# Fused attention and two dense stages: the loads of token units 2 and 3 moved behind those of units 0 and 1, into the space of the second activation tile

## The chip, the cores and the metric

The kernel runs on one core of a Trainium2 chip. The metric is the device time of one execution, in microseconds (us); less is better. Engines are named as in the profile: PE (TensorE, with PEld for its weight loads), DVE (VectorE), ACT (ScalarE), POOL (GpSimd), SP (the engine that issues all loads here), and a trailing q for an engine's sequencer (SPq).

## The reference

Inputs are r, k, v, w of 4 batches x 8 heads x 768 tokens x 48, a vector u of 8 x 48, and five weight arrays. First a recurrence over the tokens of a batch row, per head:

```python
for t in range(S):
    cur = np.einsum('bhd,bhe->bhde', u[None] * kt, vt)
    y[:, :, t] = np.einsum('bhd,bhde->bhe', rt, state + cur)
    state = wt[:, :, :, None] * state + np.einsum('bhd,bhe->bhde', kt, vt)
```

Its output, 3072 tokens x 384, goes through two dense stages:

```python
h = x @ w_in;  x = (h - np.tanh(h)) @ w_out                      # 384 -> 2048 -> 384
h = x @ w_in2; solu = h * softmax(h)                             # 384 -> 1024
out = (layernorm(solu) * g_ln) @ w_out2                          # 1024 -> 384
```

## The kernel before, in words

**Units, blocks, slices.** The recurrence is done in NU = 24 units of 128 tokens. UB = 4 units make a block of 512 tokens, the width of a matmul of the first dense stage; there are NB = 6 blocks. The first dense stage's weights are cut into NM = 16 slices.

**A unit.** `att_load` (L187) has SP load w, r, k into a tile `rkw` (L194, three loads) and v into one of four tiles `vt` (L195). There are two `rkw` tiles, so unit u + 2 is loaded once unit u has been read. `att_pre` has ACT look whether all w are in the range for which the method is safe (`check_w`, L234, two operations that use the tile `inv` as scratch), POOL multiply r, k and u (L243, L244, also in `inv`), and DVE sum (L245). `att_0` transposes w and r on PE (L260), runs four scans on DVE (L274), a logarithm and an exponential on ACT (L277, L278) and a product on DVE (L279). `att_1` has POOL multiply into `inv` (L286), PE transpose k, DVE do L287 and L288. `att_2` is a matmul (L301), a masked copy on DVE (L303, two) and a transpose (L307, copied by ACT, L308). `att_3` is a matmul (L317, L318) and the update of the running state on DVE: L327 adds the matmul's result in PSUM to the old state, L328 multiplies that by a factor, both of its inputs in SBUF. `att_4` is the output matmul (L340, L343).

**The hand-over to the dense stage.** The output of a unit goes into the block's activation tile `xs` as a high and a low part. Three quarters are written there by ACT (L345) and DVE (L347). The last quarter goes to a small tile `x3` (ACT L346, DVE L348) and from there by six SP copies (L351) to other partitions of `xs`. There is one `x3`, so the next unit's L346 waits until the six copies have landed. There are two `xs` tiles; the second is first used by unit 4.

**Weights.** `conv_a` takes a slice: SP loads a raw pair of w_in and w_out, stored as 64-bit numbers (`load_pair`: L361, L362 twice each, L366) into one of two raw buffers; ACT checks it (L121); DVE turns it into 32-bit numbers (L129, L130, L131, twice each); ACT and POOL split that into high and low parts `wa` (L134, L135).

**The dense stage.** `part1` of a block and a slice is nine matmuls `hp` (L381), then ACT L386, DVE L387 (`y`), ACT L390, DVE L392 (`y`), ACT L393, ACT or POOL a cast and POOL the low part of `g` (L398). `part2` is nine matmuls `x2p` (L405). Two PSUM banks hold `hp`.

**What sets the order.** All work is written in one program order, from which a scheduler makes each engine's queue. Until the first block is complete the order comes from a list `first` of (time, function, unit), sorted by time: stage k of unit u stands at k + 2.1 u, the loads of units 2 and on at their own times, and `conv_a` of slices 0 and 1 (`early` = 2) at 0 and 2. After that a loop over s does one `part1`, at most one stage of a unit from 4 on, one `part2` and one `conv_a` (slice s + 2) per step.

## Time and profile before

| | |
|---|---|
| three runs | 786.26, 782.85, 785.9 us (median 785.9) |
| the profiled execution | 782.14 us, of which the span is 780.3 |
| mean granted TensorE clock | 0.985 |
| PE busy | 731.3 us, 94% of the span |
| DVE, ACT, POOL busy | 582.5 (75%), 495.0 (63%), 419.7 us (54%) |
| moved by DMA | 113.12 MB, mean 145 GB/s |

The span goes from the first to the last instruction that the profile shows; the execution's own time is 1.8 us longer. A PE that is busy in nearly all of a stretch is what limits that stretch, so what matters is where PE is not busy. The 40 slices of the page are 19.5 us each; PE's digits are 3, 6, 7, 7 and 9 in the first five, and 9 in nearly all others.

### The profile page before, as it was taken

Reading aid. Unit: us, or ns where it says so; the run is one execution under the profiler, and the core shown is the slowest. Engines: PE = TensorE matmul, PEld = TensorE weight load, DVE = VectorE, ACT = ScalarE, POOL = GpSimd, SP = SyncE. Lnnn points to the kernel's source line nnn. Section 1 sums busy time; section 2 is a strip of 40 time slices with the busy share of each in tenths; the row PEclk is TensorE's granted clock in tenths of the full one; section 3 lists DMA queues with packets and bytes.
Section 4 is the critical chain, followed back from the end, with each engine's and each line's share of the span. In section 5 each row is a group of like instructions: output and inputs, shape, how many; then the busy total and the mean of one; then the engine's idle time right before and its main releaser. Section 6 shows DMA issues by size and latency. Waiting matters only on the chain. (4 is left out here: it accounts for less than half of the span.)

```text
span 780.3 us, 13211 instructions
## 1 busy us (share of the span) xinstructions
PE 731.3 (94%) x4338; PEld 605.5 (78%) x4338; DVE 582.5 (75%) x1023; ACT 495.0 (63%) x944; POOL 419.7 (54%) x389
## 2 busy tenths in 40 slices
PE   3677989899999999999999999999999999999996
PEld 2565767678887888887887887887778999998986
DVE  4688989776776677766676765468569899999992
ACT  3434777487776777686777765697745554554552
POOL 3444657466565656646555655367425444545440
PEclk9978999999999999999999999999999999999999
DMA  9964674778587568657665630043035555645531
GB/s 164 184 101 116 132 179 122 169 176 206 127 182 184 137 152 184 172 145 205 158 158 162 178 88 25 25 143 121 5 130 184 178 172 168 195 161 171 184 108 46
DMA packets 178158, 113.12 MB, mean 145 GB/s; under 512 B 95520, under 2 KB 166816, under 8 KB 178080
## 3 DMA queue, kind: packets, MB, share of 16 engines
q1 hardware_dynamic: 178080, 112.19, 55.5%
q8 instruction: 36, 0.59, 0.3%
q14 instruction: 42, 0.34, 0.1%
HBM read 88.81 MB, written 20.97 MB: 141 GB/s over the span
## 5 line engine op out<-in xcount | busy, mean ns | idle before, releaser
L405 PE MATMUL x2p<-g,wa 128*128 128x512 f32 x864 | 223.9, 398 | 4.0 <-ACT g L395 2.8
L381 PE MATMUL hp<-xs,wa 128*128 128x512 f32 x864 | 216.9, 395 | 5.5 <-DVE y L392 5.0
L381 PEld LDWEIGHTS hp<-xs,wa 128*128 128x128 f32 x864 | 162.5, 190 | 43.1 <-POOL wa L135 7.0
L405 PEld LDWEIGHTS x2p<-g,wa 128*128 128x128 f32 x864 | 158.1, 188 | 42.6 <-issue 4.2
L398 POOL TENSOR_TENSOR g<-y,g 128x512 fp32r<-128x512 f32 x96 | 128.6, 1340 | 42.7 <-ACT g L395 33.3
L387 DVE TENSOR_TENSOR y<-hp,t 128x512 f32<-128x512 f32 x96 | 65.9, 687 | 81.3 <-ACT t L386 65.5
L393 ACT ACTIVATE q<-t,cst 128x512 f32<-128x512 f32 x96 | 69.4, 723 | 65.6 <-DVE y L392 65.1
L462 PE MATMUL h<-wb,x2s 128*128 128x512 f32 x432 | 103.8, 392 | 3.0 <-POOL x2s L451 1.4
L544 PE MATMUL o<-wb,ts 128*128 128x384 f32 x576 | 105.1, 336 | 1.0 <-POOL ts L523 1.0
L544 PEld LDWEIGHTS o<-wb,ts 128*128 128x128 f32 x576 | 100.8, 188 | 3.0 <-POOL ts L523 1.3
L462 PEld LDWEIGHTS h<-wb,x2s 128*128 128x128 f32 x432 | 80.6, 188 | 20.0 <-POOL x2s L451 1.9
L397 POOL TENSOR_SCALAR g<-y 128x512 fp32r<-128x512 f32 x64 | 40.3, 630 | 91.9 <-DVE y L392 65.4
L386 ACT ACTIVATE t<-hp 128x512 f32<-128x512 f32 x96 | 56.5, 589 | 26.1 <-PE hp L381 25.4
L523 POOL TENSOR_TENSOR ts<-tw,ts 128x512 fp32r<-128x512 f32 x44 | 57.9, 1339 | 7.5 <-ACT ts L522 7.4
L392 DVE SCALAR_TENSOR_TENSOR y<-q,y 128x512 f32<-128x512 f32 x64 | 49.9, 780 | 4.4 <-ACT q L390 1.2
L451 POOL TENSOR_TENSOR x2s<-x2s 128x384 fp32r<-128x384 f32 x24 | 24.9, 1040 | 49.9 <-ACT x2s L450 49.9
L495 ACT ACTIVATE e<-so 128x1024 f32<-128x1024 f32 x24 | 25.5, 1060 | 37.2 <-DVE so L494 37.2
L390 ACT ACTIVATE q<-t,cst 128x512 f32<-128x512 f32 x64 | 46.2, 722 | 1.2
L519 DVE STREAM_TRANSPOSE tw<-sw 128x1024 f32<-128x1024 f32 x22 | 45.0, 2046 | 2.6 <-DMA sw<-dso 2.4
L286 POOL TENSOR_TENSOR inv<-inc,kh 112x512 f32<-112x512 f32 x24 | 29.7, 1236 | 32.0 <-ACT kh L278 25.9
L135 POOL TENSOR_TENSOR wa<-cv_x,wa 128x768 fp32r<-128x768 f32 x16 | 29.4, 1839 | 29.7 <-ACT wa L134 29.7
L301 PEld LDWEIGHTS qk<-rh,kh 48*128 48x128 f32 x384 | 28.0, 200 | 18.8 <-issue 12.3
(134 smaller groups left out, 1208.1 us busy)
## 6 DMA issues: line engine op xcount, KB each, us to landing
raw<-in_moe_w_out_dram SPq DMA_DIRECT2D x48, 384.0 KB, 4.4
dso<-so SPq DMA_DIRECT2D x22, 512.0 KB, 3.0
sw<-dso SPq DMA_DIRECT2D x88, 128.0 KB, 3.0
raw<-in_moe_w_in_dram SPq DMA_DIRECT2D x64, 144.0 KB, 3.6
rkw<-in_r_dram SPq DMA_DIRECT2D x64, 96.0 KB, 2.7
rkw<-in_k_dram SPq DMA_DIRECT2D x64, 96.0 KB, 2.5
rkw<-in_w_dram SPq DMA_DIRECT2D x64, 96.0 KB, 3.3
raw<-in_moe_w_in_dram SPq DMA_DIRECT2D x16, 384.0 KB, 3.6
```

The costliest lines, as they stand in the source:

```text
L381: self.mm(hp, self.wa[:, a, m, j * 128:(j + 1) * 128], xs[:, b, j], start=n == 0, stop=n == len(seq) - 1)
L386: nc.scalar.activation(t, hp, AF.Square)
L387: v.tensor_tensor(y, hp, t, ALU.mult)
L390: nc.scalar.activation(p, t, AF.Square, bias=self.c_fsb, scale=F_S)
L392: self.last_dve = v.scalar_tensor_tensor(y, p, F_E, y, ALU.add, ALU.mult)
L393: self.last_act = nc.scalar.activation(q, t, AF.Relu, bias=self.c_t2, accum_out=self.flags[:, col:col + 1])
L398: g.tensor_tensor(gs[:, 1], y, gs[:, 0], ALU.subtract)
L405: self.mm(self.x2p[d], self.wa[:, a, m, sl], gs[:, b], start=m == 0 and n == 0, stop=m == NM - 1 and n == 2)
L462: self.mm(p[:, f], xs[:, a, j], w, start=q == 0, stop=q == 8)
L519: self.turned = nc.vector.transpose(x.rearrange("p k (t b) -> p b k t", b=4), sw)
L523: nc.gpsimd.tensor_tensor(ts[:, 1, k], x[:, k], ts[:, 0, k], ALU.subtract)
L544: self.mm(p, ts[:, a, k], self.wb[:, b, k, DM:], start=q == 0, stop=q == 3 * NM2 - 1)
```

## The change

Units 0 to 3 get an `rkw` tile each: two more are made in the space in which the second `xs` tile is made later, at unit 4's `att_4` (the tag `xs1`). The loads of units 2 and 3 stand right behind those of units 0 and 1, and the raw pairs of slices 0 and 1 behind them (`K.raws`); the rest of `conv_a` of these slices moves to 4.15 and 6.25 in the list. `behind()` puts unit 4's `att_0` and `conv_a` of slices 2 and 3 behind unit 3's last operations on DVE, ACT and PE. `check_w` becomes a Square and a Relu with one flag column instead of two Relus with two, works in place on the loaded w and moves from `att_pre` to `att_0`, behind the transposes. The product of r, k and u goes to a tile of its own up to unit 4. The state update of units 0 to 3 leaves its sum in PSUM, so that the product behind it has one input there. The diff, cut to its core:

```diff
-        self.nflag = 2 * NU + NB * NM + NM + NM2
+        const.tile([128, 24], F32, name="pad")
+        self.nflag = NU + NB * NM + NM + NM2
...
-        self.xs = [xp.tile([128, 2, KM, BLK], F32R, name=f"xs{i}") for i, xp in enumerate((xp0, xp1))]
+        self.xs = [xp0.tile([128, 2, KM, BLK], F32R, name="xs0")]
+        self.xp1 = xp1
...
+        x = xp1.tile([128, 2 * RKW], F32, tag="xs1", name="rkw23")
+        self.rkw += [x[:, RKW * i:RKW * (i + 1)].rearrange("p (i h d) -> p i h d", i=3, h=H) for i in range(2)]
...
+    def behind(self):
+        st = ExitStack()
+        for i in self.last3:
+            st.enter_context(self.tc.issue_after(i.ins))
+        return st
+
+    def rk(self, u):
+        return self.rkw[u if u < UB else u % 2]
...
-        for i, (b, s) in enumerate(((self.c_lo, -1.0), (self.c_hi, 1.0))):
-            self.nc.scalar.activation(tmp, w, AF.Relu, bias=b, scale=s,
-                                      accum_out=self.flags[:, 2 * u + i:2 * u + i + 1])
+        self.nc.scalar.activation(tmp, w, AF.Square, bias=self.c_mid)
+        self.nc.scalar.activation(tmp, tmp, AF.Relu, bias=self.c_rad, accum_out=self.flags[:, u:u + 1])
...
-        if u < TURN:
-            self.check_w(u, t[:, 2, :, 0:D], self.ruk)
-        nc.gpsimd.tensor_tensor(self.ruk, r, self.ub, ALU.mult)
-        nc.gpsimd.tensor_tensor(self.ruk, k, self.ruk, ALU.mult)
+        ruk = self.ruk
+        if u <= UB:
+            ruk = self.gp.tile([128, BLK], F32, tag="y", name="ruk")[:, 0:DM].rearrange("p (h d) -> p h d", h=H)
+        nc.gpsimd.tensor_tensor(ruk, r, self.ub, ALU.mult)
+        nc.gpsimd.tensor_tensor(ruk, k, ruk, ALU.mult)
...
             pr = self._transposes(u, 0)
+            w = self.rk(u)[:, 2, :, 0:D]
+            self.check_w(u, w, w)
...
-                v.tensor_tensor(n, p[s], old[s, :, s], ALU.add)
-                v.tensor_tensor(n, n, end, ALU.mult)
+                sm = p[s] if u < UB else n
+                v.tensor_tensor(sm, p[s], old[s, :, s], ALU.add)
+                v.tensor_tensor(n, sm, end, ALU.mult)
...
+        if u == UB:
+            self.xs.append(self.xp1.tile([128, 2, KM, BLK], F32R, tag="xs1", name="xs1"))
...
+        if u == UB - 1:
+            self.last3 = self.xlo, xact, ymm
...
-        raw = self.load_pair(rpool, m)
+        raw = self.raws.pop(m, None)
+        if raw is None:
+            raw = self.load_pair(rpool, m)
...
     K.att_load(1)
+    K.att_load(2)
+    K.att_load(3)
...
-    first += [(SK * (u - 2) + 1.05, K.att_load, u) for u in range(2, UB + 2)] + [(SK * UB - 1, K.att_pre, UB)]
-    first += [(2.0 * m, lambda m: K.conv_a(cv, cvr, m), m) for m in range(early)]
+    first += [(SK * (u - 2) + 1.05, K.att_load, u) for u in range(UB, UB + 2)] + [(SK * UB - 1, K.att_pre, UB)]
+    K.raws = {m: K.load_pair(cvr, m) for m in range(early)}
+    first += [(CV0 + CV1 * m, lambda m: K.conv_a(cv, cvr, m), m) for m in range(early)]
...
-                getattr(K, f"att_{k}")(u)
+                with K.behind() if u == UB and k == 0 else nullcontext():
+                    getattr(K, f"att_{k}")(u)
...
-            K.conv_a(cv, cvr, s + early)
+            with K.behind() if s < 2 else nullcontext():
+                K.conv_a(cv, cvr, s + early)
```

In the order of the instructions three places show it; the numbers in tile names are those of buffers. SP's queue before, from unit 1's v (`vt_121`) to unit 2's v and the second raw pair:

```order
L195 DMA vt_121<-in_v_dram 128x8x48
L606 DMA gl<-in_moe_g_ln_dram 128x8x1
L361 DMA raw<-in_moe_w_in_dram 48x3x256
L362 DMA raw<-in_moe_w_in_dram 16x3x256
L361 DMA raw<-in_moe_w_in_dram 48x3x256
L362 DMA raw<-in_moe_w_in_dram 16x3x256
L366 DMA raw<-in_moe_w_out_dram 128x768
L194 DMA rkw<-in_w_dram 128x8x48
L194 DMA rkw<-in_r_dram 128x8x48
L195 DMA vt_122<-in_v_dram 128x8x48
```

And with the change, from unit 1's v on (`vt2` and `vt3` are units 2 and 3):

```order
L208 DMA vt1_122<-in_v_dram 128x8x48
L207 DMA rkw23_140<-in_w_dram 128x8x48
L207 DMA rkw23_140<-in_r_dram 128x8x48
L207 DMA rkw23_140<-in_k_dram 128x8x48
L208 DMA vt2_123<-in_v_dram 128x8x48
L207 DMA rkw23_140<-in_w_dram 128x8x48
L207 DMA rkw23_140<-in_r_dram 128x8x48
L207 DMA rkw23_140<-in_k_dram 128x8x48
L208 DMA vt3_124<-in_v_dram 128x8x48
L630 DMA gl_82<-in_moe2_g_ln_dram 128x8x1
```

Behind these rows come the raw pairs of slices 0 and 1 (five loads each), then the six w, r, k loads of units 4 and 5 and v of unit 4. What follows on SP, from v of unit 4 (again `vt0`) to the second set of copies, is:

```order
L208 DMA vt0_121<-in_v_dram 128x8x48
L371 DMA xs0_137<-x3_136 16x2x128 x6
L381 DMA raw_632<-in_moe_w_in_dram 48x3x256
L382 DMA raw_632<-in_moe_w_in_dram 16x3x256
L381 DMA raw_632<-in_moe_w_in_dram 48x3x256
L382 DMA raw_632<-in_moe_w_in_dram 16x3x256
L386 DMA raw_632<-in_moe_w_out_dram 128x768
L208 DMA vt1_122<-in_v_dram 128x8x48
L381 DMA raw_715<-in_moe_w_in_dram 48x3x256
L382 DMA raw_715<-in_moe_w_in_dram 16x3x256
L381 DMA raw_715<-in_moe_w_in_dram 48x3x256
L371 DMA xs0_137<-x3_136 16x2x128 x6
```

So the third raw pair, v of unit 5 and part of the fourth raw pair stand between the copies of units 0 and 1. On DVE, around unit 3's last operations (L347, L348), the order before is:

```order
L347 TENSOR_TENSOR xs_136<-x2p_118,xs_136 112x3x128
L348 TENSOR_TENSOR x_135<-x2p_118,x_135 112x128
L303 COPY_PREDICATED aq<-mask,qk 128x512 x2
L129 TENSOR_SCALAR cv_a<-raw 128x384 x2
...
L129 TENSOR_SCALAR cv_a<-raw 128x384 x2
L130 SCALAR_TENSOR_TENSOR cv_a<-raw,cv_a 128x384 x2
L131 ISA cv_x<-raw,cv_a 128x768 x2
L387 TENSOR_TENSOR y<-hp,t 128x512 x2
```

And with the change (L365, L366 are unit 3's last, L318 is the masked copy, L130 to L132 the conversions, L409 and L414 the two `y`):

```order
L365 TENSOR_TENSOR xs_137<-x2p_119,xs_137 112x3x128
L366 TENSOR_TENSOR x_136<-x2p_119,x_136 112x128
L289 SCALAR_TENSOR_TENSOR inc_125<-tp,zeros 112x128 x4
...
L258 TENSOR_REDUCE dg_139<-inv 128x4x2
L409 TENSOR_TENSOR y<-hp,t 128x512 x2
L318 COPY_PREDICATED aq<-mask,qk 128x512 x2
L130 TENSOR_SCALAR cv_a<-raw 128x384
L414 SCALAR_TENSOR_TENSOR y<-hp,y 128x512
L130 TENSOR_SCALAR cv_a<-raw 128x384
L414 SCALAR_TENSOR_TENSOR y<-hp,y 128x512
L131 SCALAR_TENSOR_TENSOR cv_a<-raw,cv_a 128x384 x2
```

Unit 4's scans have moved behind unit 3's last operation, and the conversions of slices 2 and 3 from ahead of the first `y` to behind it.

## Rows read from the trace of the kernel before

**Rows 1.** Windows: stretch, length, busy us and instructions of PE, PEld, DVE, ACT, POOL, PEclk, DMA share, GB/s
```profile
0.00:66.70 66.70, 38.44 (x352) 31.06 (x352) 44.10 (x98) 26.39 (x55) 30.29 (x40) 0.90 0.83 142
66.70:165.00 98.30, 88.26 (x509) 67.92 (x509) 84.28 (x171) 69.83 (x132) 58.29 (x43) 0.97 0.61 147
165.00:780.00 615.00, 604.57 (x3480) 506.57 (x3478) 454.17 (x756) 398.80 (x758) 331.09 (x306) 1.00 0.52 145
```

**Rows 2.** Windows, the first 40 us, same columns
```profile
0.00:20.00 20.00, 6.61 (x26) 4.72 (x27) 9.25 (x30) 6.87 (x12) 7.71 (x20) 1.00 0.99 166
20.00:40.00 20.00, 13.35 (x134) 10.97 (x134) 12.05 (x26) 9.59 (x19) 10.06 (x9) 1.00 0.99 175
```

**Rows 3.** Line L195 in 8 to 9 us, v of unit 1: durations, start, time to landing
```profile
L195 SPq DMA_DIRECT2D vt<-in_v_dram x1: 1007/1007/1007, 8.5 to 8.5; - x1
...
DMA to landing us min/median/max: 5.4/5.4/5.4
```

**Rows 4.** Line L366 in 13 to 14 us, the first raw pair's last load
```profile
L366 SPq DMA_DIRECT2D raw<-in_moe_w_out_dram x1: 422/422/422, 13.5 to 13.5; - x1
...
DMA to landing us min/median/max: 3.7/3.7/3.7
```

**Rows 5.** Line L194 in 14 to 15 us, w and r of unit 2
```profile
L194 SPq DMA_DIRECT2D rkw<-in_w_dram x1: 384/384/384, 14.0 to 14.0; - x1
...
L194 SPq DMA_DIRECT2D rkw<-in_r_dram x1: 517/517/517, 14.5 to 14.5; - x1
...
DMA to landing us min/median/max: 4.4/4.7/5.1
```

**Rows 6.** Line L351 in 34 to 36 us, copies of unit 0 behind loads
```profile
L351 SPq DMA_DIRECT2D xs<-x x3: 616/800/996, 34.0 to 35.7; - x3
...
DMA to landing us min/median/max: 3.4/3.9/4.7
```

**Rows 7.** Line L351 in 63 to 67 us, copies of unit 3
```profile
L351 SPq DMA_DIRECT2D xs<-x x6: 586/592/597, 63.3 to 66.5; - x6
...
DMA to landing us min/median/max: 1.8/2.2/3.5
```

**Rows 8.** Timeline of ACT: start, us, operation, in brackets the idle time before it
```profile
61.19 0.27 ACT L346 CAST x<-x2p 112x128 fp32r<-112x128 f32 x1 [1.30 <-DMA xs<-x]
```

**Rows 9.** Timeline of PE, the first matmuls of slices 0 and 1, then of slice 2
```profile
66.73 5.97 PE L381 MATMUL hp<-xs,wa 128*128 128x512 f32 x18
...
77.33 2.99 PE L381 MATMUL hp<-xs,wa 128*128 128x512 f32 x12 [1.70 <-DVE y L392]
```

**Rows 10.** Timeline of DVE around the first matmuls of the dense stage
```profile
62.97 0.28 DVE L348 TENSOR_TENSOR x<-x2p,x 112x128 fp32r<-112x128 f32 x1
64.24 1.34 DVE L303 COPY_PREDICATED aq<-mask,qk 128x512 f32<-128x512 uint8 x2 [0.99 <-PE qk L301]
...
70.39 1.01 DVE L129 TENSOR_SCALAR cv_a<-raw 128x384 uint32<-128x384 uint32 x2
...
73.17 1.28 DVE L387 TENSOR_TENSOR y<-hp,t 128x512 f32<-128x512 f32 x2
75.23 1.37 DVE L274 TENSOR_TENSOR_SCAN inc<-tp,zeros 112x128 f32<-112x128 f32 x4 [0.78 <-PE tp L260]
...
77.10 0.68 DVE L279 TENSOR_TENSOR rh<-tp,inc 112x512 f32<-112x512 f32 x1
77.69 0.55 DVE L129 TENSOR_SCALAR cv_a<-raw 128x384 uint32<-128x384 uint32 x1
78.16 0.68 DVE L392 SCALAR_TENSOR_TENSOR y<-hp,y 128x512 f32<-128x512 f32 x1
```

**Rows 11.** Waits of DVE in 73 to 165 us: total, times, longest
```profile
DVE inc L274 <- PE tp L260: 1.8, 2, 1.0
...
DVE st L327 <- PE ds L318: 0.4, 1, 0.4
```

**Rows 12.** Groups of DVE in 0 to 66 us: busy us, mean ns, idle before
```profile
L328 DVE TENSOR_TENSOR st<-st,inc 48x192 f32<-48x192 f32 x6 | 5.3, 882 | 0.2
...
L327 DVE TENSOR_TENSOR st<-ds,st 48x192 f32<-48x192 f32 x4 | 1.4, 353 | 1.0 <-PE ds L318 0.9
```

More of the change, by code (lines that the diff above doesn't have):

```diff
@@ L34 @@
 TURN = 2 * UB
-W_LO, W_HI = 0.75, 1.34
+W_MID, W_RAD2 = 1.045, 0.087025
 P_MIN = 1e-30
@@ L77, in setup @@
         nc.vector.memset(self.zeros, 0.0)
-        for i, val in enumerate((F_SB, -F_T2, W_LO, -W_HI, -0.5, P_SB, P_MIN, FLAG_MIN2)):
+        for i, val in enumerate((F_SB, -F_T2, -W_MID, -W_RAD2, -0.5, P_SB, P_MIN, FLAG_MIN2)):
             nc.vector.memset(self.cst[:, i:i + 1], val)
-        (self.c_fsb, self.c_t2, self.c_lo, self.c_hi, self.c_mhalf, self.c_sb, self.c_min,
+        (self.c_fsb, self.c_t2, self.c_mid, self.c_rad, self.c_mhalf, self.c_sb, self.c_min,
          self.c_flag) = (self.cst[:, i:i + 1] for i in range(8))
@@ L146, in check_pair @@
         with self.tc.issue_after(self.last_act.ins):
-            self.check(raw, 2 * NU + NB * NM + n)
+            self.check(raw, NU + NB * NM + n)
     def load_pair(self, rpool, n):
@@ L190, in att_load @@
         b, c = divmod(u, NC)
-        t = self.rkw[u % 2]
+        t = self.rk(u)
         sl = slice(c * C, (c + 1) * C)
@@ L232, in check_w @@
     def check_w(self, u, w, tmp):
-        for i, (b, s) in enumerate(((self.c_lo, -1.0), (self.c_hi, 1.0))):
-            self.nc.scalar.activation(tmp, w, AF.Relu, bias=b, scale=s,
-                                      accum_out=self.flags[:, 2 * u + i:2 * u + i + 1])
+        self.nc.scalar.activation(tmp, w, AF.Square, bias=self.c_mid)
+        self.nc.scalar.activation(tmp, tmp, AF.Relu, bias=self.c_rad, accum_out=self.flags[:, u:u + 1])
     def att_pre(self, u):
         nc = self.nc
-        t = self.rkw[u % 2]
+        t = self.rk(u)
         r, k = (t[:, 0, :, 0:D], t[:, 1, :, 0:D]) if u < TURN else (self.nat[:, 0], self.nat[:, 1])
-        if u < TURN:
-            self.check_w(u, t[:, 2, :, 0:D], self.ruk)
-        nc.gpsimd.tensor_tensor(self.ruk, r, self.ub, ALU.mult)
-        nc.gpsimd.tensor_tensor(self.ruk, k, self.ruk, ALU.mult)
-        nc.vector.reduce_sum(self.dg[u % 2].rearrange("p e j -> p j e"), self.ruk.rearrange("p (j e) d -> p j e d", e=2), axis=AX)
+        ruk = self.ruk
[3 more added lines that the diff above has]
+        nc.gpsimd.tensor_tensor(ruk, k, ruk, ALU.mult)
+        nc.vector.reduce_sum(self.dg[u % 2].rearrange("p e j -> p j e"), ruk.rearrange("p (j e) d -> p j e d", e=2), axis=AX)
     def bank(self, u, name):
@@ L259, in _transposes @@
         for j in range(4):
-            self.nc.tensor.transpose(p[:, j], self.rkw[u % 2][:, i, 2 * j:2 * j + 2, :], self.ident)
+            self.nc.tensor.transpose(p[:, j], self.rk(u)[:, i, 2 * j:2 * j + 2, :], self.ident)
         return p
@@ L342, in att_4 @@
                 h = 2 * j + e
-                self.mm(p[64 * e:64 * e + m, j], vt[:, h * D:h * D + m], self.aq[:, e, j], start=first, stop=True)
+                ymm = self.mm(p[64 * e:64 * e + m, j], vt[:, h * D:h * D + m], self.aq[:, e, j], start=first, stop=True)
         xs, x3 = self.xs[blk % 2], self.x3
         nc.scalar.copy(xs[:NP, 0, :, cols], p[:NP, 0:3])
-        nc.scalar.copy(x3[:NP, 0], p[:NP, 3])
+        xact = nc.scalar.copy(x3[:NP, 0], p[:NP, 3])
         v.tensor_tensor(xs[:NP, 1, :, cols], p[:NP, 0:3], xs[:NP, 0, :, cols], ALU.subtract)
-        v.tensor_tensor(x3[:NP, 1], p[:NP, 3], x3[:NP, 0], ALU.subtract)
+        self.xlo = v.tensor_tensor(x3[:NP, 1], p[:NP, 3], x3[:NP, 0], ALU.subtract)
+        if u == UB - 1:
+            self.last3 = self.xlo, xact, ymm
         for j in range(KM):
@@ L390, in part1 @@
         nc.scalar.activation(p, t, AF.Square, bias=self.c_fsb, scale=F_S)
-        col = 2 * NU + i * NM + m
+        col = NU + i * NM + m
         self.last_dve = v.scalar_tensor_tensor(y, p, F_E, y, ALU.add, ALU.mult)
@@ L610, in fast_path @@
     SK = 2.1
+    CV0, CV1 = 4.15, 2.1
     first = [(k + SK * u, K.att_pre if k < 0 else getattr(K, f"att_{k}"), u) for u in range(UB) for k in range(-1, 5)]
-    first += [(SK * (u - 2) + 1.05, K.att_load, u) for u in range(2, UB + 2)] + [(SK * UB - 1, K.att_pre, UB)]
-    first += [(2.0 * m, lambda m: K.conv_a(cv, cvr, m), m) for m in range(early)]
+    first += [(SK * (u - 2) + 1.05, K.att_load, u) for u in range(UB, UB + 2)] + [(SK * UB - 1, K.att_pre, UB)]
+    K.raws = {m: K.load_pair(cvr, m) for m in range(early)}
+    first += [(CV0 + CV1 * m, lambda m: K.conv_a(cv, cvr, m), m) for m in range(early)]
     for _, f, n in sorted(first, key=lambda e: e[0]):
```

## The prediction

> **What bounds the kernel now.** I read the windows first. From 165 us to the end PE is busy 604.57 of 615 us; between 66.7 and 165 it is idle for 98.3 - 88.26 = 10.0 us, and before 66.7 for 66.7 - 38.44 = 28.3 us [rows 1]. So after 165 us nothing in this change can gain more than crumbs; what it can win is idle PE time in the first 165 us, 38.3 us in all. The point to watch is 66.73 us, where PE starts the first matmul of the dense stage [rows 9]: until then it has only the recurrence's small matmuls.
>
> Why is it not earlier? The finer windows show DMA at 0.99 in both of the first 20 us stretches, with DVE and PE about half idle [rows 2]. SP's loads land one after another: unit 1's v at 8.46 + 5.4 = 13.9 us [rows 3], the first raw pair's last load at 13.49 + 3.7 = 17.2 [rows 4], w and r of unit 2 at 14.03 + 4.4 = 18.4 and 14.52 + 5.1 = 19.6 [rows 5]. That gives two prices: a load of 192 KB takes 19.6 - 18.4 = **1.2 us** of the stream, a raw pair 17.2 - 13.9 = **3.3 us** (a tiny load is in that). Unit 2 thus waits for raw pair 0, and unit 3, by the order, for pairs 1 to 3. These raw pairs aren't needed before the first block is complete.
>
> **The change, part by part.**
>
> *The loads.* By SP's order the eight loads of units 2 and 3 now follow 13.9: 13.9 + 8 x 1.2 = 23.5. Two raw pairs: 30.1. Seven loads (units 4 and 5): 38.5. Behind these stand the first six copies from `x3`, about 0.2 us each in a full stream: in the row the first of three, issued at 34.0, takes 4.7 us and the third, issued 1.7 us later, 3.4, so they land within 0.4 us [rows 6]. The copies of unit 0 are in at about 38.5 + 1.2 = 39.7.
>
> *The chain of copies.* There is one `x3`. ACT's write of it waits for the six copies of the unit before, as it does for 1.30 us at unit 3 now [rows 8]. A round is therefore ACT 0.27 and DVE 0.28, then six issues, the last 3.2 us after the first, and its landing, 2.2: 0.27 + 0.28 + 3.2 + 2.2 = 6.0 us [rows 7, 8, 10]. In round 1 the queue is longer than that: raw pair 2, v of unit 5, half of raw pair 3 and the copies, 3.3 + 1.2 + 1.6 + 1.2 = 7.3, so 39.7 + 7.3 = 47.0. In round 2 what is ahead (half a pair, one load, six copies) is under 6 us, so 47.0 + 6.0 = 53.0. Unit 3's `x3` is then complete at 53.0 + 0.55 = 53.6, and its second copy, which the first matmul needs, lands 0.6 + 2.2 us after: first matmul at **about 56.5**, 10.2 us earlier than 66.73. DVE can keep up: it is busy 44.1 us up to 66.7 [rows 1], some 6 of it on work of units 4 and 5 and slices 2 and 3 that now comes later.
>
> *What is put behind.* The 18 matmuls of slices 0 and 1 take 5.97 us [rows 9], so they end at 62.5. Now DVE's order matters: the two `y` of L387, the masked copies, the conversions of slices 2 and 3, the two L392 and unit 4's state update all stand behind them. Prices from rows 10: the last `y` ends 0.6 + 0.7 after the matmuls (ACT's square, taken like `y`, and half of 1.28); masked copies 1.34; conversion 73.17 - 70.39 = 2.78 per slice, 5.56 for two; L392 2 x 0.68; state update four times 0.355 [rows 12], 1.4. Together 11.0, so DVE is through with this set at 62.5 + 11.0 = 73.5. Before, it was through with the same set at 78.16 + 0.68 = 78.8, and in that time it had also done a part of unit 5 and slice 4 that now comes later, 1.37 + 0.68 + 0.55 = 2.6 [rows 10]: it stood at 76.2. DVE's lead is **2.7 us**, not 10.2. PE's third slice needs L392 and the converted weights, so PE's lead shrinks to the same order, about 2.5.
>
> *Afterwards.* Between 73 and 165 us DVE waits for PE or ACT in six rows of the waits, 6.2 us together, of which the first and the last are shown [rows 11]. PE, which is ahead of its conversions now, should spare some of it. Bounds: 0 and 6.2; I take 2, since the largest, for transposes and the score matmul, come when PE has just been given late work. Sum: -2.5 - 2 = **-4.5 us**.
>
> *The state update.* L328 has 0.355 us of work like L327, yet its six take 5.3 us against 1.4 for four of L327, whose one input is in PSUM [rows 12]. The excess, 5.3 - 6 x 0.355 = 3.2 us, lies on DVE before 66 us. With the chain of copies as the bound, DVE would only wait longer for the copies, so I count 0; bounds 0 and -3.2. The Trainium skill ("SBUF — State Buffer", "Who interferes with whom") says that a DVE operation with two SBUF inputs contends with a GpSimd one that reads SBUF, and one with at most one does not; by it the edit removes all of the 3.2 us, and the trace's slow L328 against L327 speaks for it. By it the sum would be up to -7.7, if DVE and not the copies set the end.
>
> *Costed at nothing.* The check's second operation and its move (ACT is busy 26.4 of 66.7 us, hidden by the DMA wait); the products' own tile (POOL 30.3 of 66.7) [rows 1]; and four more clearing operations on POOL, at the mean of its 20 in the first 20 us, 7.71 / 20 = 0.39, 1.5 us [rows 2], while the loads are under way. If that cover is gone, they delay the head by 1.5 us at most, where 10.2 us are gained and 2.7 used.
>
> **To the number.** The profiled execution took 782.1 us, the other runs 782.85 to 786.26 (median 785.9). Own time: 782.1 - 4.5 = 777.6; from the median 781.4. I use the mean of the four known executions, 784.3, as what a new one would show: **779.8**. A measurement of this kernel can tell about 0.5%, 3.9 us, from no change.
>
> **The rivals.**
>
> *A, the forecast:* gain 2 to 7.5 us (777 to 782). *Chance 0.50.* The start of 56.5 may be off by 2 either way, and the share of 6.2 us is a guess.
>
> *B, the lead is kept.* The scheduler's interleaving lets PE do slice 2's and unit 4's matmuls in the shadow of the conversions, the state update sheds its 3.2 us, and PE's idle 10 us after 66.7 [rows 1] shrink as well: 7.5 to 11 us, about **775**. For it: 38.3 us of idle PE lie before 165 us. Against: 11.0 us of DVE work stand behind the first matmuls. *0.18.*
>
> *C, nothing comes of it.* The conversions, and behind them POOL's low part of the weights, come so late that slices 2 and 3 start at 77.33 as now [rows 9]; PE then merely waits there instead of at 66.7: within 2 us, about **784**. For it: PE already waits there for L392. *0.18.*
>
> *D, slower.* Mechanism: SP issues raw pair 2 and half of 3 between the copies of units 0 and 1, and these wait for a raw buffer, that is for DVE's conversions of slices 0 and 1, which now come late in its order. While SP waits, the copies behind wait too. Landing in a full queue costs 4.7 against 1.8 us [rows 6, 7]. If the conversion of slice 0 ends 5 us after the copies of unit 0 are issued, and that of slice 1 again, the start moves from 56.5 to about 66.5, and with 11.0 us behind it DVE's set is through at 66.5 + 6.0 + 11.0 = 83.5 against 76.2: 7 us late, of which waits give back about 1: 784.3 + 6 = **790**. It decides from a first matmul later than 76.2 - 11.0 - 6.0 = 59.2, or 61 with the 2 us of waits. Against it: raw pair 0 is in at 26.8, so DVE should have converted it by 33. *0.14.* [...]
>
> That the change doesn't do what it says is out: the orders show loads, scans and conversions in their new places.
>
> **How the numbers follow.** Faster by over 0.5% takes B (0.18) and about two thirds of A (0.32): 0.50. Same takes the rest of A and C and a little of D: 0.38. Slower, the rest of D: 0.12. The range of 8 in 10 runs from 771, inside B with the state update's 3.2 us in full, to 787, which leaves most of D out; A alone is 777 to 782.
>
> **What would show it.** The first `hp` near 56.5; DMA at 0.99 up to about 40 us; ACT's write of `x3` at units 1 to 3 waiting for copies; the state product at some 0.36 us each; DVE's conversion of slices 2 and 3 ending near 73; the third slice's matmul between 73 and 76; PE idle before 165 us down from 38.3 to about 34. I'd be wrong if the copies did not set the pace of units 1 to 3, if SP waits for raw buffers ahead of them, or if PE's lead of 10 us survives the conversions.

## The result, and the profile after

| | before | after |
|---|---|---|
| median, range | 784.38 us (779.92 to 786.26, 4 runs) | **793.35 us** (792.41 to 794.26, 4 runs) |
| ratio | | 1.0132, 95% interval 1.01 to 1.0165 |
| the profiled execution, its span | 782.14, 780.3 us | 793.33, 791.6 us |
| mean granted TensorE clock | 0.985 | 0.973 |
| PE, DVE, ACT busy | 731.3, 582.5, 495.0 us | 737.2, 587.6, 492.8 us |
| first matmul of the dense stage (L381, now L403) | 66.7 us | 61.3 us |
| first matmul of the second block | 164.6 us | 173.5 us |

The change makes the kernel **slower by 1.3%**. The last two rows tell where: the dense stage starts 5.4 us earlier, yet its first block (144 `hp` matmuls) lasts 112.2 us instead of 97.8. From the second block on PE is idle for 10.4 us in either kernel. Within the first block, 9.1 of the 14.4 us are lost between the first matmul and the third slice (19.7 us instead of 10.6), the other 5.2 from there to the second block.

A correction to the part above: L121 (now L122) does not check the raw pair. It scales the low words in place, and the third DVE operation of the conversion (L131, now L132) needs it. So ACT stands in the conversions' chain.

PE's timeline after, which answers to [rows 9] (start, us, operation, in brackets the idle time before it):

```profile
61.29 6.90 PE L403 MATMUL hp<-xs,wa 128*128 128x512 f32 x18 [5.91 <-DMA xs<-x]
72.54 0.96 PE L427 MATMUL x2p<-g,wa 128*128 128x512 f32 x3
...
80.99 2.21 PE L403 MATMUL hp<-xs,wa 128*128 128x512 f32 x9
...
92.24 1.65 PE L427 MATMUL x2p<-g,wa 128*128 128x512 f32 x3 [5.64 <-ACT g L417]
```

The third slice starts at 80.99, 3.7 us later than the 77.33 of before: the lead is gone by then. PE's waits (total us, times, longest) in 66 to 175 us after, that is up to the end of its first block:

```profile
PE x2p L427 <- ACT g L417: 13.2, 5, 5.6
PE ds L332 <- ACT kn L323: 2.1, 1, 2.1
```

and before, in 66 to 165 us:

```profile
PE hp L381 <- DVE y L392: 5.0, 4, 2.3
PE x2p L405 <- ACT g L395: 2.8, 3, 1.2
```

So PE now waits for ACT's cast of `g`, without which `x2p` can't start. What does ACT do meanwhile? Its timeline after:

```profile
93.60 0.61 ACT L417 CAST g<-y 128x512 fp32r<-128x512 f32 x1
97.24 0.92 ACT L122 ACTIVATE raw<-raw 128x768 uint32<-128x768 uint32 x1 [3.03 <-DMA raw<-in_moe_w_out_dram]
100.50 0.90 ACT L122 ACTIVATE raw<-raw 128x768 uint32<-128x768 uint32 x1 [2.34 <-DMA raw<-in_moe_w_out_dram]
101.30 0.58 ACT L408 ACTIVATE t<-hp 128x512 f32<-128x512 f32 x1
...
105.54 0.62 ACT L417 CAST g<-y 128x512 fp32r<-128x512 f32 x1 [1.64 <-DVE y L414]
```

An engine works through its queue in order: between the casts of 93.60 and 105.54, ACT stands twice in front of a raw pair that has not landed, and `t`, `y` and the cast of the next slice stand behind it. ACT's waits in 66 to 170 us, before and then after:

```profile
ACT raw L121 <- DMA raw<-in_moe_w_out_dram: 15.4, 10, 3.7
ACT t L386 <- PE hp L381: 5.6, 8, 1.1
```

```profile
ACT raw L122 <- DMA raw<-in_moe_w_out_dram: 17.4, 10, 3.0
ACT t L408 <- PE hp L403: 11.7, 7, 6.8
```

ACT waits longer than before for PE, which waits for ACT, and a little longer for raw pairs (2.0 us more).

A queue stops in order on DVE too, in the head. Its timeline after:

```profile
41.02 0.56 DVE L365 TENSOR_TENSOR xs<-y,xs 112x384 fp32r<-112x384 f32 x1 [1.72 <-ACT x L364]
...
50.13 0.56 DVE L365 TENSOR_TENSOR xs<-y,xs 112x384 fp32r<-112x384 f32 x1 [3.79 <-ACT x L364]
...
56.83 0.56 DVE L365 TENSOR_TENSOR xs<-x2p,xs 112x384 fp32r<-112x384 f32 x1 [2.77 <-ACT x L364]
...
57.50 1.36 DVE L289 TENSOR_TENSOR_SCAN inc<-tp,zeros 112x128 f32<-112x128 f32 x4
```

Three times DVE waits for the round of `x3` and its copies, and unit 4's scans come right after the last of them, at 57.50; before they stood at 54.0, ahead of unit 2's hand-over. The windows add it up. Columns as in [rows 1]; first before, then after:

```profile
40.00:61.30 21.30, 15.07 (x164) 12.56 (x158) 18.45 (x35) 7.82 (x20) 10.52 (x10) 0.76 0.57 95
61.30:90.00 28.70, 24.40 (x159) 19.51 (x159) 25.15 (x54) 19.49 (x41) 14.89 (x12) 0.88 0.66 139
90.00:165.00 75.00, 67.28 (x389) 51.21 (x388) 63.48 (x127) 52.45 (x98) 45.40 (x35) 0.98 0.61 148
```

```profile
40.00:61.30 21.30, 10.66 (x133) 9.34 (x133) 11.56 (x26) 7.24 (x15) 4.50 (x4) 0.82 0.60 135
61.30:90.00 28.70, 22.77 (x134) 17.70 (x134) 20.47 (x43) 13.90 (x27) 9.97 (x8) 0.85 0.35 86
90.00:165.00 75.00, 65.48 (x378) 50.20 (x379) 60.00 (x119) 50.03 (x93) 46.15 (x35) 0.91 0.64 154
```

From 40 to 90 us DVE does 32.0 us of work instead of 43.6, ACT 21.1 instead of 27.3. Not all of that is undone work. Up to 40 us DVE had done more than before (26.0 instead of 21.3 us). The whole stretch up to the first matmul of the dense stage, before and then after, is:

```profile
0.00:61.30 61.30, 35.02 (x316) 28.25 (x316) 39.75 (x89) 24.28 (x50) 28.29 (x38) 0.92 0.84 144
0.00:61.30 61.30, 34.49 (x317) 28.19 (x317) 37.58 (x92) 23.81 (x45) 28.57 (x42) 0.88 0.91 151
```

DVE is 2.2 us short there, less than the 3.2 us that the state update saves; ACT is 0.5 us short, and POOL and PE are level. So by busy time no engine is behind at 61.3 us. The arrears come from 61.3 to 90 us: DVE does 4.7 us less than before in that stretch, ACT 5.6, POOL 4.9. At its start ACT and DVE stand in front of the first `hp` and the first `y`:

```profile
67.54 1.29 ACT L408 ACTIVATE t<-hp 128x512 f32<-128x512 f32 x2 [6.82 <-PE hp L403]
68.17 1.38 DVE L409 TENSOR_TENSOR y<-hp,t 128x512 f32<-128x512 f32 x2 [2.71 <-ACT t L408]
...
78.17 1.02 DVE L132 CUSTOM_DVE_ANT_0 cv_x<-raw,cv_a 128x768 uint16<-128x768 uint16 x2
```

The raw pairs of slices 2 and 3 had landed at 45.2 and 52.6, but their conversions stand behind that `y` and end at 79.2. Before, they ended at 73.2, ahead of the first `y`. From 90 to 165 us neither engine catches up; both do less than before.

### The profile page after: what moved, and what is told of

Its sections match the earlier page's. It is cut to its first block, busy times and chain, and to the rows that moved or that the text cites. A ratio compares the mean times of both kernels' runs of the same rounds, so it can differ in the third digit from the quotient of the medians.

```text
span 791.6 us, 13209 instructions
## 1 busy us (share of the span) xinstructions
PE 737.2 (93%) x4338; PEld 609.6 (77%) x4338; DVE 587.6 (74%) x1023; ACT 492.8 (62%) x920; POOL 420.7 (53%) x393
## 4 chain that ended last, share of the span: by engine, by line
PE 72%; DVE 7%; ACT 7%; SPq 6%; DMA 5%; issue 2%; POOL 1%; ACTq 0%; DVEq 0%
PE hp L403 20%; PE x2p L427 19%; PE o L566 12%; PE h L484 11%; DMA raw<-in_moe_w_out_dram 3%; PE qk L316 3%; PE y L361 2%; PE y L358 2%; SPq L207 2%; SPq L371 2%; DVE cv_x L132 2%; ACT raw L122 1%; DMA xs<-x 1%; PE kt L322 1%; PE ds L332 1%
## 5 line engine op out<-in xcount | busy, mean ns | idle before, releaser
L427 PE MATMUL x2p<-g,wa 128*128 128x512 f32 x864 | 227.3, 401 | 14.5 <-ACT g L417 13.2
L403 PE MATMUL hp<-xs,wa 128*128 128x512 f32 x864 | 221.9, 402 | 6.3 <-DMA xs<-x 5.9
L403 PEld LDWEIGHTS hp<-xs,wa 128*128 128x128 f32 x864 | 166.5, 194 | 44.1 <-ACT kh L293 6.1
L409 DVE TENSOR_TENSOR y<-hp,t 128x512 f32<-128x512 f32 x96 | 65.9, 686 | 83.0 <-ACT t L408 71.5
L484 PE MATMUL h<-wb,x2s 128*128 128x512 f32 x432 | 105.4, 396 | 3.3 <-POOL x2s L473 1.8
L415 ACT ACTIVATE q<-t,cst 128x512 f32<-128x512 f32 x96 | 69.2, 721 | 61.6 <-DVE y L414 61.1
L414 DVE SCALAR_TENSOR_TENSOR y<-q,y 128x512 f32<-128x512 f32 x64 | 52.3, 818 | 3.7 <-ACT q L412 0.2
L361 PE MATMUL y<-aq,vt 128*48 128x128 f32 (+1 forms) x368 | 40.5, 283 | 0.0
```

The lines of the kernel that those rows point to most:

```text
L361: ymm = self.mm(p[64 * e:64 * e + m, j], vt[:, h * D:h * D + m], self.aq[:, e, j], start=first, stop=True)
L403: self.mm(hp, self.wa[:, a, m, j * 128:(j + 1) * 128], xs[:, b, j], start=n == 0, stop=n == len(seq) - 1)
L409: v.tensor_tensor(y, hp, t, ALU.mult)
L414: self.last_dve = v.scalar_tensor_tensor(y, p, F_E, y, ALU.add, ALU.mult)
L415: self.last_act = nc.scalar.activation(q, t, AF.Relu, bias=self.c_t2, accum_out=self.flags[:, col:col + 1])
L427: self.mm(self.x2p[d], self.wa[:, a, m, sl], gs[:, b], start=m == 0 and n == 0, stop=m == NM - 1 and n == 2)
```

## The experiments

Each kernel is timed against the kernel before on the same chip. Block 1 is the first matmul of the second block, and unit 7 the landing of its last copy; both in the profiled execution. The first matmuls of block 1 need only the first of unit 7's copies, so in nine rows block 1 starts up to 2.5 us ahead of the last one. The kernel before was timed anew beside each group, so the ratios are what is compared; medians of different groups can be off against each other by 2 us.

| kernel | ratio to before, 95% interval | median us | block 1 | unit 7 |
|---|---|---|---|---|
| before | 1 | 782.0 to 784.4 | 164.6 | 164.3 |
| the change | 1.0132 [1.01, 1.0165] | 793.35 | 173.5 | 170.9 |
| e1 conversions not behind | 1.0105 [1.0071, 1.014] | 791.24 | 173.3 | 173.1 |
| e2 unit 4 not behind | 1.0046 [1.0018, 1.0074] | 786.14 | 172.0 | 172.5 |
| e3 neither behind | 1.0101 [1.0071, 1.013] | 790.39 | 173.0 | 172.7 |
| e4 early loads alone | 1.0041 [1.002, 1.0061] | 787.57 | 168.5 | 169.4 |
| e5 small edits alone | 1.0003 [0.9981, 1.0024] | 783.54 | 164.3 | 164.9 |
| e14 all but the early loads | 1.0187 [1.016, 1.0213] | 798.96 | 181.3 | 179.3 |
| e6 slices 2, 3 need no weights of their own | 1.0112 [1.0054, 1.017] | 791.14 | 170.7 | 170.7 |
| e8 no slice of block 0 does | 1.0111 [1.0068, 1.0154] | 791.21 | 173.3 | 175.1 |
| e9 before, conversions 2, 3 late | 1.0215 [1.0165, 1.0264] | 800.28 | 183.2 | 185.4 |
| e11 change, conversions in the head | 1.0188 [1.0143, 1.0233] | 796.47 | 175.7 | 177.5 |
| e12 the same, later in it | 1.0175 [1.0131, 1.0219] | 796.37 | 177.0 | 179.5 |
| e20 change, conversions ahead of unit 4 | 1.0149 [1.0108, 1.0189] | 793.75 | 178.9 | 180.5 |
| e22 e20 with the old loads | 1.0197 [1.015, 1.0245] | 797.7 | 180.9 | 182.7 |
| e13 change, no raw loads from slice 4 on | 0.9975 [0.9955, 0.9995] | 781.14 | 163.0 | 162.9 |
| e15 before, no raw loads from slice 4 on | 0.9978 [0.9954, 1.0002] | 780.78 | 156.7 | 155.0 |
| e25 change, units 5 to 7 earlier | 1.0095 [1.0062, 1.0128] | 790.59 | 170.1 | 153.6 |
| e26 before, units 5 to 7 earlier | 1.0012 [0.9987, 1.0036] | 783.62 | 170.4 | 153.0 |
| e29 e25, unit 4 not behind | 1.0027 [1.0004, 1.005] | 784.87 | 165.1 | 148.8 |

A profiled execution is one of several: e2's was the slowest of its ten (790.16 us), so its ratio is read and not its block 1. e15's too was the slowest of its ten (782.81; the others from 776.32 on).

### Which part of the change costs the time

e1, e2 and e3 take the waits of `behind()` away, from the conversions, from unit 4, from both:

```diff
-            with K.behind() if s < 2 else nullcontext():
+            with nullcontext():
                 K.conv_a(cv, cvr, s + early)
```

```diff
-                with K.behind() if u == UB and k == 0 else nullcontext():
+                with nullcontext():
                     getattr(K, f"att_{k}")(u)
```

> The changed kernel, with slices 2 and 3's conversions no longer put behind unit 3's last operations; unit 4's first stage still is. Theory P (the loss comes from the place of these two conversions on DVE: slices 2 and 3 get their weights late, so PE spends the 18 + 18 matmuls x2p of slices 0 and 1 before it and then has nothing to do while slice 2 goes through ACT, DVE and POOL): the scheduler still leaves both conversions behind the first y here and puts 12 of the 18 x2p ahead of slice 2, so 790 to 795 us as the changed kernel, slice 2's hp near 81. Theory Q (the loss comes from unit 4's first stage being late): also 790 to 795, so this run does not tell P from Q. Theory W (the wait itself of behind() on the conversions is the cost): 781 to 787.

> The changed kernel, with unit 4's first stage no longer put behind unit 3's last operations; the conversions still are. In the order both conversions now stand ahead of the first y on DVE, and slice 2's hp ahead of the first x2p on PE. P: slice 2's hp near 72, no wait of 5 us of x2p for g before 95 us, 778 to 785 us. Q: a gain as well, 780 to 787. W: 790 to 795.

> The changed kernel without behind() at all: loads, check, products and state sums as changed. Conversions stand ahead of the first y, 18 hp of slices 2 and 3 ahead of the x2p of 0 and 1. P and Q: 776 to 785 us, so that the early loads alone are worth something against the kernel before. If the head is no better than before by itself (theory R: the copies through the one x3 set the pace whatever the loads do): 783 to 788, first hp at 61 or later.

Freeing the conversions gives 2 us, inside the uncertainty. Freeing unit 4 gives 7.2 us (793.35 to 786.14; 0.9% between the ratios), and the intervals stand apart: **while the conversions are queued, most of the loss goes when unit 4's stage is not.** That is not the price of unit 4's place alone: in e2 the conversion of slice 2 also ends earlier, at 65.2 instead of 75.5. Freeing both does not add up: 790.39, outside every range given for it, and against e1 freeing unit 4 then gives nothing (1.0105 and 1.0101). What the waits buy shows in the first `hp`: it comes at 61.3 in the change, 63.5 in e2, 64.3 in e1, and 66.5 in e3, where the copies of unit 3 land at 68.9 instead of 62.7.

e4 leaves only the early loads (e3 without the new check, the products' tile and the PSUM sum), e5 is the kernel before with those small edits, e14 is e5 with both waits of `behind()`, that is the change without its early loads.

> The kernel before with the loads of the change alone: four tiles for units 0 to 3, the early loads, the two raw pairs behind them, conversions of slices 0 and 1 at 4.15 and 6.25; check, products, state sum and queueing as before. Around unit 3 its DVE order is that of the kernel before. Theory L (the early loads by themselves make block 0 worse, since units 4 and 5 and the raw pairs come in another order): 788 to 793 as without behind(). Theory M (the small edits, the check in place and the others, do it): 779 to 784.

> The kernel before with the small edits alone: check as Square and Relu in place behind the transposes, product in its own tile, state sum in PSUM; loads and queueing as before. L: 780 to 785. M: 787 to 793.

> The kernel before with the small edits and both uses of behind(), and with the loads as they were. If behind() is the bulk of the loss: 788 to 796, the first hp not earlier than 64, block 0 near 112 us. If the early loads are needed for the loss: 780 to 786.

The small edits are worth nothing. The early loads by themselves cost 0.4% (787.57, between its two forecasts). They do not bring the dense stage forward: the first `hp` of e4 comes at 66.6, as before. With the old loads the two waits cost 1.9%, more than its forecast; with the early loads they and all else cost 1.3% (798.96 and 793.35; the two intervals just overlap). The parts are not additive, and a rule for one holds only with the others named.

### Is it the late weights of slices 2 and 3?

The first theory: the conversions behind the first `y` make slices 2 and 3 wait. e6 and e8 let the matmuls use weights that are ready, with all conversions still done where the change puts them (e6 in `hp` of slices 2 and 3, e8 in `hp` and `x2p` of the whole first block; both leave out the right weights there). The first of e8's two lines:

```diff
-            self.mm(hp, self.wa[:, a, m, j * 128:(j + 1) * 128], xs[:, b, j], start=n == 0, stop=n == len(seq) - 1)
+            self.mm(hp, self.wa[:, a, m % 2 if i == 0 else m, j * 128:(j + 1) * 128], xs[:, b, j], start=n == 0, stop=n == len(seq) - 1)
```

> The changed kernel, but in block 0 the hp of slices 2 and 3 use the weights of slices 0 and 1, so that they wait for no late conversion; all conversions, loads and the same number of matmuls are still there, and unit 4's first stage is still late. P: slice 2's hp right behind unit 4's score matmuls near 72, and most of the 9 to 11 us come back: 781 to 787 us. Q: unchanged, 790 to 795.

> The changed kernel, but in all of block 0 both matmul stages use the weights of slices 0 and 1, so that PE waits for no weights there; all loads and conversions are still done. Theory S (block 0 is paced by the supply of weights: with two raw buffers a pair is loaded only when the conversion of the pair two before is over, so a late conversion of slices 2 and 3 shifts everything to slice 15; in four kernels it took 88.6 to 90.0 us from the end of slice 3's conversion on DVE to slice 15's last weights on POOL): PE is freed from it, 780 to 786 us, slice 15's hp before 165. Against S (the pace is set by ACT and DVE themselves, in whose queues raw checks and conversions stand): 789 to 794, slice 15's hp at 168 to 172.

The theory falls: 791.1 and 791.2. In e6 slice 2 starts at 71.8 instead of 81.0, and the second block only 2.8 us earlier than in the change. In e8, whose time is that of "against S" though its slice 15 is not, the last slice of block 0 is done much earlier, and PE then waits for unit 7 (timeline of PE, e8):

```profile
144.78 2.35 PE L403 MATMUL hp<-xs,wa 128*128 128x512 f32 x9 [0.88 <-DVE y L414]
155.34 4.29 PE L427 MATMUL x2p<-g,wa 128*128 128x512 f32 x9 [5.69 <-ACT g L417]
173.34 2.90 PE L403 MATMUL hp<-xs,wa 128*128 128x512 f32 x6 [6.38 <-DMA xs<-x]
```

Before, slice 15 of block 0 starts at 161.9, after at 170.0, in e8 at 144.8; the second block at 164.6, 173.5 and 173.3.

e9 does the opposite: in the kernel before it puts conversions 2 and 3 behind the first two slices' last DVE operation.

```diff
-            K.conv_a(cv, cvr, s + early)
+            with tc.issue_after(K.last_dve.ins) if s < 2 else nullcontext():
+                K.conv_a(cv, cvr, s + early)
```

> The kernel before, with one edit: the conversions of slices 2 and 3 are put behind the last y of slices 0 and 1. S: slice 3's conversion ends near 82 instead of 73.2, slice 15's weights come about 9 us later, near 171, and the time is 7 to 10 us longer, 789 to 792. Against S: within 3 us of before, 780 to 785, since no other work is changed.

That costs 2.2% (800.28), 8 us above S's range. So late conversions can cost 2% where unit 4 is on time (its scans at 54.3); the later units are not, with unit 5's scans at 86.4 instead of 75.2. In the change the conversions are not the only thing that is late. The next four bring them forward instead: e11 and e12 write conversions 2 and 3 into the list of the head (at 6.25 and 7.3, or 8.2 and 9.3), e20 puts them right behind unit 3 and unit 4's stage behind them, e22 does that with the old loads.

```diff
-    early = 2
+    early = 4
...
-    first += [(CV0 + CV1 * m, lambda m: K.conv_a(cv, cvr, m), m) for m in range(early)]
+    first += [((CV0, CV0 + CV1, 6.25, 7.3)[m], lambda m: K.conv_a(cv, cvr, m), m) for m in range(early)]
```

```diff
+    first += [(10.35 + 0.05 * m, conv_b3, m) for m in range(2, early)]
...
-                with K.behind() if u == UB and k == 0 else nullcontext():
+                with tc.issue_after(K.last_cv.ins) if u == UB and k == 0 else nullcontext():
```

> The changed kernel with the conversions of slices 2 and 3 written into the list of the first block at 6.25 and 7.3 (behind unit 1's last operations, ahead of unit 2's), so that they run while DVE waits for the copies, and raw pairs 4 and 5 are asked for ahead of units 2 and 3's copies. S: slice 3's conversion ends near 57, 16 us earlier than before, the weights are no longer the pace, and PE is: 771 to 778 us; the raw pairs ahead of the copies may cost 2 to 5 of it. Against S: no faster than the kernel before, 782 to 790.

> As the run before, with the two conversions at 8.2 and 9.3 in the list: around unit 2's last operations, with half of the raw pairs 4 and 5 behind unit 2's copies. S: slice 3's conversion ends near 58, first hp near 62: 771 to 778 us. Against S: 782 to 790.

> The changed kernel, with the conversions of slices 2 and 3 directly behind unit 3's last operations, unit 4's first stage behind these, and the conversions of slices 4 and 5 free. Theory O (what costs is that the two conversions stand behind unit 4's first stage and the first y): slice 3's conversion ends near 64 instead of 79, raw pairs 4 and 5 are asked for near 64, first hp near 61, 774 to 782 us. Against O (a late unit 4 or the early loads cost by themselves): 786 to 793.

> The same order of conversions and of unit 4's first stage, with the small edits and the loads as in the kernel before. O: like the kernel before or a little faster, 777 to 785 us, first hp near 65, slice 3's conversion ending near 68; with the early loads of e20 worth 3 to 4 us more. Against O: 788 to 799, as in the run with behind() and the old loads.

No theory's range was met; e22 alone lies in a range, the one against O. e11, e12 and e20 are slower than even the ranges against the theories. In e12 conversion 3 ends at 58.0 and in e20 at 63.0 (79.2 in the change), and neither is faster than the change: the units come later instead (unit 5's scans at 95.1 and 89.9 against 83.8 in the change and 75.2 before, unit 7's copies in at 179.5 and 180.5).

### Is it the wait for raw pairs?

e13 is the change, e15 the kernel before, in which slices 4 to 15 convert the raw pair that lies in the buffer again and load none:

```diff
-            raw = self.load_pair(rpool, m)
+            raw = self.keep[m % 2] if m > 3 else self.load_pair(rpool, m)
```

> The changed kernel, but slices 4 to 15 convert again the raw pairs that are in the two buffers and load none: the same conversions on ACT, DVE and POOL, 12 raw pairs less moved. Theory S2 (in the changed kernel ACT and DVE stand still in block 0 because the raw pairs 4 and on are asked for late, and what is queued behind, y, g and units 4 to 7, is late by it): 775 to 783 us, block 0 (from the first hp to the first of block 1) at most 102 us long instead of 112. Against S2 (the order of the work itself, and the lower clock after each gap): 787 or more, block 0 at least 107 us.

> The kernel before, with slices 4 to 15 converting again the raw pairs in the two buffers, 12 raw pairs less moved (the control of the same edit in the changed kernel, which gained 12 us). Theory S2 (the late conversions of slices 2 and 3 make the raw pairs late; the kernel before has little of this): at most 5 us faster, 778 to 784. Theory G (raw pairs limit both kernels alike): 10 us or more faster, 768 to 774.

**In the time the whole loss is gone**: 0.9975 against 0.9978. For the kernel before the edit is worth nothing that can be measured there, for the change 12 us. Both outcomes are those of S2. The windows of e13 show how:

```profile
40.00:61.30 21.30, 10.97 (x133) 9.65 (x133) 11.49 (x26) 7.24 (x15) 4.44 (x4) 0.82 0.61 135
61.30:90.00 28.70, 23.61 (x136) 18.10 (x137) 20.27 (x43) 15.25 (x30) 11.57 (x10) 0.84 0.20 37
90.00:165.00 75.00, 72.13 (x417) 54.83 (x415) 70.20 (x137) 57.46 (x106) 50.79 (x39) 0.98 0.28 63
```

Up to 90 us DVE and ACT are as far behind as in the change (DVE 11.49 and 20.27, ACT 7.24 and 15.25). From 90 to 165 us DVE then does 70.20 us of work against 60.00, ACT 57.46 against 50.03: they catch up. PE's wait for the cast of `g` in the first block, 13.2 in the change, shrinks (66 to 165 us) to

```profile
PE x2p L429 <- ACT g L419: 3.8, 3, 2.5
```

The control is less clean than its time. In the first block the same edit helps the kernel before almost as much: its block shrinks from 97.8 to 91.2 us and its second block starts 7.9 us earlier (156.7), against 112.2 to 101.7 us and 10.5 us for the change (163.0). Of the 8.9 us by which the change starts its second block late, 6.2 are left when neither kernel waits for raw pairs, so in this block theory G holds better than S2. e15 then loses its lead at the third block, where unit 11's copies are not in yet (PE's timeline of e15):

```profile
242.94 1.06 PE L383 MATMUL hp<-xs,wa 128*128 128x512 f32 x3 [3.20 <-DMA xs<-x]
```

The granted clock of 200 to 300 us is 0.95 there instead of 1.00, and by the fourth block e15 is where the kernel before is (330.2 and 329.9). So the two runs show that the change without raw loads is as fast as the kernel before. They do not show that the waits for raw pairs are the whole difference.

A pair's load is issued when one of the two raw buffers has been converted. In the change pair 4's last load is issued at 77.3 instead of 72.3 and pair 7's at 94.7 instead of 90.2, and the low part of slice 15's weights starts at 167.3 instead of 160.0. That looks like a stream that keeps its delay to the end, but an early pair 4 does not bring slice 15 forward: in e12 it is issued at 61.1 and in e20 at 63.0, and slice 15's low part still starts at 164.5 and 165.9.

### Is it the late units 4 to 7?

By then, over 17 kernels, the second block started within 3 us of unit 7's landing. So the theory U: the chain of units 4 to 7, made late by queueing unit 4, sets the time. e25 writes units 5 to 7 two steps earlier in the change, e26 does it in the kernel before, e29 also frees unit 4.

```diff
-    OFF = -18
+    OFF, SH = -18, 2
...
-            if rem == 0 and UB <= u < NU:
+            if rem == 0 and (u == UB or TURN <= u < NU):
...
+            u, rem = divmod(s + SH - OFF - d, 4)
+            if rem == 0 and UB < u < TURN:
+                getattr(K, f"att_{k}")(u)
```

> The changed kernel, with the stages of units 5 to 7 (and what of them stands ahead of the projections) written two steps earlier in the loop over the slices; unit 4's stage and the conversions of units 2 and 3 stay queued where the change put them. U (the recurrence of units 4 to 7, put late by the change, is the chain that sets when the second block starts, and with it the time): unit 5's scans come at some 60 us instead of 83.8, the copies of unit 7 land by 165 us or before instead of 170.9, and the time is 780 to 787 us. Against U (the gaps of the first block come from the loads and conversions, whatever the units do): the time stays at 790 to 795 us though unit 5 is early.

> The kernel before with the same shift of two steps for units 5 to 7. U: unit 5's scans come ahead of 75.2 us, unit 7's copies land ahead of 164.3 us, and the time is 776 to 783 us, at or under the kernel before. Against U: the same time or slower, 782 to 790 us.

> As the first of these runs, and unit 4's stage is no longer queued behind unit 3's last operations: units 2 and 3 loaded early, units 4 to 7 early, conversions of units 2 and 3 ahead of the first y. U: unit 7's copies land by 163 us or before, 774 to 783 us. Against U: 785 us or more.

**U falls in this form.** In e25 unit 5's scans come at 61.1 and unit 7 is in at 153.6, 17 us earlier than in the change, but the time is 790.59, as "against U" had it. The end of block 0 is now held up elsewhere: PE waits 3.81 us for the cast of `g`, and the `y` that this cast needs stands on DVE behind the conversion of slice 15, for whose raw pair DVE has stood 3.76 us (PE's timeline, then DVE's).

```profile
155.10 2.20 PE L403 MATMUL hp<-xs,wa 128*128 128x512 f32 x9
162.48 5.68 PE L427 MATMUL x2p<-g,wa 128*128 128x512 f32 x12 [3.81 <-ACT g L417]
168.00 4.29 PE L403 MATMUL hp<-xs,wa 128*128 128x512 f32 x18
```

```profile
156.60 0.56 DVE L130 TENSOR_SCALAR cv_a<-raw 128x384 uint32<-128x384 uint32 x1 [3.76 <-DMA raw<-in_moe_w_in_dram]
157.07 0.68 DVE L409 TENSOR_TENSOR y<-hp,t 128x512 f32<-128x512 f32 x1
```

So unit 7 alone does not set the second block, though the two had gone together in all those kernels. e8 took the wait for weights from PE and met unit 7 at 173; e25 brought the units forward and met the raw pairs, with the second block at 170. e26 missed too (783.62, no faster than before, with its second block at 170.4), and e29 (784.87) lies between its two forecasts. But e25 to e29 repeats e2: freeing unit 4 gives 5.7 us, and again the intervals don't touch; again slice 2's conversion comes earlier with it (66.4 instead of 75.8). No version that computes the result beat the kernel before.

### What is shown and what is open

Shown: while the conversions are queued, the queueing of unit 4's stage costs 6 to 7 us (two pairs); the small edits nothing; without raw loads from slice 4 on the time of the change is that of the kernel before (e13); and bringing either the weights or the units forward does not lift the loss. The arrears of ACT and DVE arise from 61.3 to 90 us, behind the first matmuls, and not in the head. My reading, that ACT and DVE can't make them up later since their queues keep stopping at raw pairs, is borne out by e13, in which they do catch up; but e15 shows that the stops cost the kernel before nearly as much in its first block, and the share of each stop was not measured by itself. So the cause is narrowed down and not shown. Open: why the early loads cost 0.4% by themselves (e4), where unit 5 is on time but unit 6's scans are 5.2 us late (105.6 against 100.4), and why freeing the conversions beside unit 4 loses part of what freeing unit 4 gains (e3 against e2). A clearing of both chains at once, and a third raw buffer, were not tried.

## Why the prediction was wrong

| step | forecast | measured |
|---|---|---|
| unit 3's v landed | 23.5 | 23.6 |
| two raw pairs landed | 30.1 | 31.7 |
| v of unit 4 landed | 38.5 | 38.8 |
| copies of units 0, 1, 2 landed | 39.7, 47.0, 53.0 | 40.7, 49.7, 56.4 |
| first `hp` | 56.5 | 61.3 |
| conversions 2, 3 done | DVE's set at 73.5 | 79.2 |
| third slice | 73 to 76 | 81.0 |
| time | 779.8 (771 to 787) | 793.35 |

**The loads** were right to within 2 us; so were the price of 1.2 us and the claim that copies then set the pace.

**The rounds of copies** were sized too small: 9.0 and 6.7 us for units 1 and 2 against 7.3 and 6.0, and 4.9 against 3.5 from unit 2's landing to the first `hp`. The first `hp` came 4.8 us later than forecast. That puts it at the point that rival D named, 61, and D's number was near (790), but not by its mechanism: raw pair 0 was converted by 32 and the queue did not stop for it. The lateness was in the rounds themselves. Two things were left out of them: in round 1 SP also has to issue the nine loads between the copies, from 39.6 to 44.1 us, before the first copy; and in each round DVE's L365 (0.56 us, the rows above) stands ahead of DVE's write to `x3`.

**The failed step is "Afterwards", -2 us.** Its bounds, 0 and 6.2, were both a gain; a loss was excluded without a reason. The change reached the third slice 3.7 us late and the second block 8.9 us late, so this stretch lost 5.2 us where 2 were to be won. That is 7.2 of the 15.8 us between the forecast of -4.5 and the spans' 11.3. The rounds of copies are 4.8 of it. From the first `hp` to the third slice the forecast was nearly right (18.3 us, measured 19.7), which is 1.4. What follows the second block, forecast as unchanged, is 2.4 (a second block 0.8 faster, and 3.2 slower after it).

"DVE's lead is 2.7 us" did not come true since the start was late, but its sum held: DVE was to be through 11.0 us behind the 18 matmuls, and these end at 68.2 and its last conversion at 79.2. What the step "Afterwards" lacked:

- It looked at DVE's waits alone. ACT was not balanced at all; it is the engine that PE waits for in the change (13.2 us, 2.8 before), and it was 6 us behind at 90 us.
- Slices 4 and on need raw pairs, and each pair waits for a raw buffer, that is for conversions 2 and 3, which the change had just put late. From the third slice to the second block the change takes 92.5 us and the kernel before 87.2; without raw loads from slice 4 on, 81.8 (e13) and 79.1 (e15). About half of the 5.2 us thus goes with these loads; the rest stays open.
- The [rows 1] window of 66.7 to 165 us shows PE idle 10.0 us; I took this as what could be won. It was also the stretch that could get longer.

**Costed at nothing** was right: e5 shows it, with the old loads. The state update did get faster, as forecast, and it bought nothing, as the sum had it. In the groups of DVE up to 66 us, which answer to [rows 12]:

```profile
L343 DVE TENSOR_TENSOR ds<-ds,st 48x192 f32<-48x192 f32 x4 | 1.5, 367 | 0.4 <-PE ds L333 0.3
L344 DVE TENSOR_TENSOR st<-ds,inc 48x192 f32<-48x192 f32 x4 | 1.4, 355 | 0.1
```

The product now takes 355 ns instead of 882. The rule of the Trainium skill ("SBUF — State Buffer", "Who interferes with whom"), that a DVE operation with at most one input in SBUF does not contend with GpSimd, agrees with that. The sum that it would have given, -7.7, needed DVE to be the bound, and DVE waited for copies instead.

**The chances.** Slower by over 0.5% had 0.12, all of it in a rival whose place was wrong. A rival for "the first block itself gets longer behind an earlier start" was missing.

## What to carry to other kernels

An edit that lets a stage start earlier by pushing work out of its way has to be charged for that work on every engine, up to the point where both kernels have done the same set, and not at the first milestone: here the milestone improved by 5.4 us and the block behind it lost 14.4. Idle time in front of a wait is a place to put work, so an ordering that empties it ("behind the last operation of ...") needs a reason why the later stretch has room; look there for in-order queues that stop at loads. Where two chains end together, clearing one may gain nothing: here the raw pairs and the units each took over when the other was brought forward. And a control is to be read by stages as well as by its time: e15's first block gained 6.6 us that its time does not show.
